# Small attention matmuls packed four at a time into PE tiles, in a linear-attention and MLP block

## The chip, the cores and the metric

One core of a Trainium2 chip. The metric is the device time of one execution in microseconds (us). Single executions are quoted as the median of a kernel's runs. "PE" is TensorE, "PEld" its weight loads, "DVE" VectorE, "ACT" ScalarE, "POOL" GpSimd, "SP" SyncE.

## The reference

The input is 2048 tokens of 640 features, bf16. After a layer norm, two branches are added to the input: a linear attention with 32 heads of 20 features, and a gated MLP with 1536 hidden features.

```python
q, k, v = split(xn @ wqkv)                       # 32 heads of 20
pq = einsum("bhsd,hdf->bhsf", q, w_phi); pk = same of k
phi_q = concat([softmax(pq), softmax(-pq)])      # 40 features a head
phi_k = concat([softmax(pk), softmax(-pk)])
kv  = einsum("bhsf,bhsd->bhfd", phi_k, v)        # the key-value sums, over all tokens
z   = einsum("bhsf->bhf", phi_k)
num = einsum("bhqf,bhfd->bhqd", phi_q, kv)       # the attention products
den = einsum("bhqf,bhf->bhq", phi_q, z)[..., None] + 1e-6
out = x + (num / den) @ wo + (silu(xn @ w1) * (xn @ w3)) @ w2
```

Two steps are awkward for matmuls of 128 x 128 tiles (the 128*128 of the page): both `kv` and `num` are 32 independent products of width 20, in two signs.

## The kernel before

A small scheduler, run while the program is built, records every instruction through one helper (hence one source line, L101, in all profile lines; L105 in the changed kernel) and fixes the order on each engine. MLP chunks (10 matmuls of 512 columns, 2.16 us of PE) fill PE wherever the attention has to wait.

The key-value sums take three heads as the stationary operand (63 columns, with a column of ones per head for `z`) in two column tiles of the array, 120 moving columns each. What is not on the diagonal of heads is thrown away later by a mask, after PE transposes have turned the result.

```python
def kv_sum(pairs, k):
    for n, p in enumerate(pairs):
        groups = [g for g in (2 * p, 2 * p + 1) if 3 * g < H]
        for t in range(T):                       # 16 token tiles of 128
            for g in groups:
                q, nh = g % 2, min(3, H - 3 * g)
                o = PS[64 * q:64 * q + 21 * nh, ...]       # column tile q
                mm(o, v2[:, t, 63 * g:63 * g + 21 * nh],
                   ekt[:, t, :, 60 * g:60 * g + 20 * nh], t == 0, t == T - 1, ...)
    ...                                          # copies to stg

def kv_store(chunks, k):
    ...
            tr(PSb[:, c:c + 128], stg[:, sg, 128 * fc:128 * fc + 128])   # PE transposes
    ...                                          # masked into KVc by DVE

def q_tok(t, k):                                 # attention products of one token tile
    for sg in range(2):
        for fc in range(DC):                     # 5 chunks of 128 features
            ...
                    mm(bank(k + 2 * sg + q, 22 * (hi - lo), ...),
                       EqT[b % 2][:, sg, fc, 128 * j:128 * j + 128],
                       KVc[:, sg, fc, ...], ...)           # full array, 154 or 88 columns
```

The softmax here doesn't subtract the row's maximum and nothing guards it: scores larger than these inputs give would overflow.

## Time and profile before

276.78 us median of 3 runs (276.57 to 276.87); the profiled execution spans 274.9 us.

First the head of the profile's page for the kernel before: busy time of PE and DVE, PE's busy tenths in 40 slices of the span, the instruction queue (packets, MB, share), and the head of the chain of waits.

```profile
span 274.9 us, 4782 instructions
PE 268.9 (98%) x1961; PEld 163.3 (59%) x1961; DVE 181.9 (66%) x318; ACT 108.1 (39%) x197; POOL 60.5 (22%) x93
PE   6999999999999999999999999999999999999996
q8 instruction: 15, 0.25, 0.4%
PE 81%; DMA 7%; DVE 5%; SPq 2%; ACT 2%; issue 1%; POOL 1%
```

PE is never out of work after the start, and in the order of time the chain is PE alone from 49.6 to 272.4 us. So a change is worth what it takes out of PE's time, or puts into it.

PE's timeline of the kernel before around the two steps: start us, length us, engine, line, operation, output<-inputs, shapes, count, and in brackets idle time before, if any.

```profile
85.60 4.96 PE L101 MATMUL PS<-ekt,v 128*63 128x120 bf16 x176
90.59 0.51 PE L101 MATMUL PS<-ident,stg 128*128 128x128 bf16 x6
90.94 2.32 PE L101 MATMUL PS<-xnT,w_s 128*128 128x512 bf16 x10
93.10 0.39 PE L101 MATMUL PS<-ident,stg 128*128 128x128 bf16 x4
93.32 8.80 PE L101 MATMUL PS<-xnT,w_s 128*128 128x512 bf16 x40
101.95 0.86 PE L101 MATMUL PS<-KVc,EqT 128*128 128x154 bf16 x12
102.65 2.32 PE L101 MATMUL PS<-xnT,Wqp 128*128 128x512 bf16 x10
```

Take starts, not lengths: matmuls overlap (at 512 columns each is 379 ns long and they start 216 ns apart), so what one group costs is the time to the next group's start. The key-value sums with their ten transposes cost 5.65 us: from 85.51, when the next ordinary matmul would have started, to 90.94, and 93.10 to 93.32. The attention products of one tile cost 102.65 - 101.95 = 0.70 us, 11.2 us for 16 tiles.

### The profile page before, as it was taken

What the parts mean: (1) busy time and instruction counts of PE and PEld (TensorE: products, weight loads), DVE (VectorE), ACT (ScalarE), POOL (GpSimd) and SP (SyncE); (2) the same over time, 40 slices, a digit from 0 to 9 for tenths busy, and PEclk for the clock granted to TensorE, in tenths of its full rate; (3) what the DMA queues carried; (4) which work ended last, traced back from release to release, by engine and by line L of the source; (5) the groups of instructions that cost most, each with busy time, mean ns of one, the idle gap of its engine ahead of it and who ended that gap; (6) DMA issues with size and microseconds to landing.
All of it is one profiled execution on the core that took longest, in us unless ns stands there. A gap on an engine that the chain in (4) does not pass through costs nothing.

```text
span 274.9 us, 4782 instructions
## 1 busy us (share of the span) xinstructions
PE 268.9 (98%) x1961; PEld 163.3 (59%) x1961; DVE 181.9 (66%) x318; ACT 108.1 (39%) x197; POOL 60.5 (22%) x93
## 2 busy tenths in 40 slices
PE   6999999999999999999999999999999999999996
PEld 2656666676447555555555455567446777777774
DVE  5459869999764698999899799978963121111112
ACT  2567987987821335445554544411320000000000
POOL 4404493999984100000000000000000000000000
DMA  7971899650000731111112111232300212121211
GB/s 202 296 223 37 176 244 295 115 145 0 0 0 2 222 117 24 25 24 26 24 31 43 24 25 26 49 46 52 93 5 0 89 56 82 61 84 61 81 42 48
DMA packets 40326, 21.96 MB, mean 80 GB/s; under 512 B 26736, under 2 KB 40304, under 8 KB 40304
## 3 DMA queue, kind: packets, MB, share of 16 engines
q1 hardware_dynamic: 40304, 21.66, 31.9%
q8 instruction: 15, 0.25, 0.4%
q14 instruction: 7, 0.06, 0.1%
HBM read 12.81 MB, written 2.62 MB: 56 GB/s over the span
## 4 chain that ended last, share of the span: by engine, by line
PE 81%; DMA 7%; DVE 5%; SPq 2%; ACT 2%; issue 1%; POOL 1%
PE PS L101 81%; DMA wqkT<-in_A_wqkv_dram 4%; DVE bst L101 3%; DMA x_tok<-in_A_x_dram 3%; SPq L113 2%; ACT x_tok L101 1%; DVE mv L101 1%; POOL rstd L101 1%; ACT ekt L101 0%; DVE Wkp L101 0%; DVE hT L101 0%; DVE t L101 0%; ACT v L101 0%; DVE xres L101 0%; DVE x_tok L101 0%
## 5 line engine op out<-in xcount | busy, mean ns | idle before, releaser
L101 PE MATMUL PS<-xnT,w_s 128*128 128x512 bf16 x480 | 107.2, 379 | 0.1
L101 PEld LDWEIGHTS PS<-xnT,w_s 128*128 128x128 bf16 x480 | 46.8, 98 | 55.1 <-ACT Wkp L101 0.3
L101 PE MATMUL PS<-w_s,hT 128*128 128x320 bf16 (+2 forms) x384 | 54.9, 299 | 0.0
L101 DVE TENSOR_TENSOR xres<-PS,xres 128x640 bf16<-128x640 f32 (+2 forms) x17 | 13.4, 786 | 54.0 <-PE PS L101 54.0
L101 ACT ACTIVATE th<-PS 128x512 f32<-128x512 f32 x48 | 28.7, 598 | 46.8 <-PE PS L101 46.8
L101 PEld LDWEIGHTS PS<-w_s,hT 128*128 128x128 bf16 x384 | 37.6, 98 | 14.6
L101 DVE SCALAR_TENSOR_TENSOR t<-th,PS 128x512 bf16<-128x512 f32 x48 | 32.7, 682 | 15.4 <-ACT th L101 15.4
L101 POOL TENSOR_TENSOR ekt<-ekt,rS 128x640 bf16<-128x640 bf16 x32 | 39.4, 1271 | 4.1 <-DVE rS L101 4.1
L101 DVE SCALAR_TENSOR_TENSOR hT<-t,PS 128x512 bf16<-128x512 bf16 x48 | 33.0, 687 | 1.7
L101 PE MATMUL PS<-wv,xnT 128*128 128x320 bf16 x160 | 24.7, 299 | 1.0 <-ACT xnT L101 1.0
L101 ACT ACTIVATE EqT<-PS 128x512 bf16<-128x512 f32 x40 | 21.7, 595 | 9.9 <-PE PS L101 9.9
L101 PE MATMUL PS<-wo_s,oT 128*128 128x320 bf16 (+2 forms) x160 | 24.5, 299 | 0.0
L101 DVE TENSOR_TENSOR prod<-PS,g_s 128x1280 bf16<-128x1280 f32 x16 | 23.9, 1491 | 0.5
L101 PE MATMUL PS<-Wkp,xnT 128*128 128x320 bf16 x160 | 23.9, 299 | 0.1
L101 PE MATMUL PS<-xnT,Wqp 128*128 128x512 bf16 x100 | 23.7, 379 | 0.0
L101 ACT ACTIVATE ekt<-PS 128x640 bf16<-128x640 f32 x32 | 20.8, 717 | 6.0 <-PE PS L101 6.0
L101 DVE TENSOR_REDUCE S<-ekt 128x64 f32<-128x1280 bf16 x16 | 23.0, 1441 | 0.0
L101 PEld LDWEIGHTS PS<-wv,xnT 128*128 128x128 bf16 x160 | 15.2, 98 | 7.5 <-ACT xnT L101 1.5
L101 PEld LDWEIGHTS PS<-Wkp,xnT 128*128 128x128 bf16 x160 | 15.4, 98 | 6.4 <-ACT ekt L101 0.3
L101 PEld LDWEIGHTS PS<-wo_s,oT 128*128 128x128 bf16 x160 | 15.6, 98 | 6.1
L101 DVE BATCH_NORM_STATS2 bst<-x_tok 128x6 f32<-128x320 bf16 x32 | 15.3, 478 | 5.8 <-DMA x_tok<-in_A_x_dram 5.2
L101 ACT ACTIVATE e_s<-PS 128x64 f32<-128x64 f32 x32 | 9.1, 283 | 22.0 <-PE PS L101 21.0
(53 smaller groups left out, 162.4 us busy)
## 6 DMA issues: line engine op xcount, KB each, us to landing
w_s<-in_B_w_dram SPq DMA_DIRECT2D x6, 640.0 KB, 6.7
xres<-in_A_x_dram SPq DMA_DIRECT2D x16, 160.0 KB, 2.4
out_dram<-xres SPq DMA_DIRECT2D x15, 160.0 KB, 1.8
x_tok<-in_A_x_dram SPq DMA_DIRECT2D x3, 640.0 KB, 6.2
w_s<-in_B_w_dram SPq DMA_DIRECT2D x1, 1920.0 KB, 8.0
wv<-in_A_wqkv_dram SPq DMA_DIRECT2D x2, 400.0 KB, 4.6
wo_s<-in_A_wo_dram SPq DMA_DIRECT2D x1, 800.0 KB, 4.7
x_tok<-in_A_x_dram SPq DMA_DIRECT2D x4, 160.0 KB, 2.9
```

Source lines behind the costliest of these rows:

```text
L101: o = _Op(eng, lambda: m(*args, **kw), r, w, cost)
L113: o = _Op(eng, lambda: m(out, in_), self.regions(in_), self.regions(out), nbytes, True)
```

## The change

The intent: give each 32-wide piece of work its own quarter of the array, so that four small matmuls run at once (as in the warm-up of the kernel before, where the four of a group start within 9 to 15 ns and each is 186 to 199 ns long in the profile) and nothing off the diagonal of heads is computed. The query features are permuted when the folded weight is written, so that 8 heads (160 features) lie as five blocks in each 32-row strip. The key-value sums of a head are one matmul of 21 x 40 in one of four 32-column tiles; one DVE 32 x 32 block transpose turns all of them and replaces the ten PE transposes. Small schedule edits go with it: the products of a token tile wait until the transposes of earlier tiles' results are at most two behind, and those transposes get priority.

```diff
+        if which:
+            evac(Wkp[...], bank2(k, 320))
+        else:
+            evac(Wqp[:, dc, :].rearrange("p (i b r j) -> p b r i j", b=2, r=2, j=32), ...)   # permuted
-    def kv_sum(pairs, k):
...
+    def kv_sum(k):
+        for n in range(8):
             for t in range(T):
+                for r in range(4):
+                    h = 8 * r + n
+                    o = PS[32 * r:32 * r + DH + 1, k * 512 + 40 * n:k * 512 + 40 * n + 40]
+                    mm(o.rearrange("p (s f) -> p s f", s=2), v2[:, t, 21 * h:21 * h + DH + 1],
+                       ekt[:, t, :, DH * h:DH * h + DH], t == 0, t == T - 1, ...)
...
+    def kv_store():
+        P.op("DVE", "transpose", [o], [i], (o, i), cost=0.5)
+        ...                                      # five masked products into KVc, for ten transposes and 15 products
     def q_tok(t, k):
         for sg in range(2):
-            for fc in range(DC):
-                ...
+            for i in range(DC):
+                for r in range(4):
+                    mm(bank(k + r, 22 * n, 176 * sg + 22 * h0),
+                       EqT[b % 2][32 * r:32 * r + 32, sg, i, 128 * j:128 * j + 128],
+                       KVc[32 * r:32 * r + 32, sg, i, 0:22 * n], ...)
```

The sums go from 176 matmuls to 512, the products from 12 a tile to 40. Each matmul is two PE instructions, a weight load and a matmul (1961 of each in the page before).

More of the change, by code (lines that the diff above doesn't have):

```diff
@@ L22, with heads_of_strip @@
 GRAN = 32
+def heads_of_strip(i):
+    return (32 * i) // DH, (32 * i + 31) // DH
 def heads_of_chunk(c):
@@ L288, in bass_parallel_sum__linear_kernel_hedgehog__glu_gated_swiglu__prompt_kernel @@
     den_s = new("den_s", [128, 2, H], f32)
-    g_s = new("g_s", [128, 2, 2, H], f32)
+    g_s = new("g_s", [128, 2, 4, 2, 8], f32)
     S64 = new("S64", [128, 3, 64], f32)
@@ L328, in bass_parallel_sum__linear_kernel_hedgehog__glu_gated_swiglu__prompt_kernel @@
     wqkT = new("wqkT", [128, 2 * DC, D], bf, RW)
-    KVc = new("KVc", [128, 2, DC, 9 * 22], bf, RW)
-    stg = new("stg", [128, 2, D], bf, RW + 3968)
-    prod = new("prod", [128, 2, 2, D], bf, RW + 3968)
+    KVc = new("KVc", [128, 2, DC, 3 * 22], bf, RW)
+    stg = new("stg", [128, 2, 160], bf, RW + 1344)
+    kvT = new("kvT", [128, 2, DC, 32], bf, RW + 1984)
+    SM = new("SM", [128, DC, 8], bf, RW + 2624)
+    prod = new("prod", [128, 2, 4, 2, 160], bf, RW + 3968)
     o_tok = new("o_tok", [128, 3, D], bf, RW + 9088)
@@ L434, in consts_late @@
         memset("POOL", eps[:, 0:1], 0.0)
-        for p in (20, 41, 62, 84, 105, 126):
-            select(eps[:, 0:1], -p, [[0, 1]], 1, ALU.not_equal, DEN_EPS / 2)
+        for r in range(4):
+            select(eps[:, 0:1], -32 * r - DH, [[0, 1]], 1, ALU.not_equal, DEN_EPS / 2)
         memset("POOL", v2[:].rearrange("p t (h c) -> p t h c", c=21)[:, :, :, DH], 1.0)
@@ L503, in fold_mm @@
                     first[q] = False
-        dst = (Wqp, Wkp)[which]
-        evac(dst[:, dc, :].rearrange("p (b c) -> p b c", c=320), bank2(k, 320))
+        if which:
+            evac(Wkp[:, dc, :].rearrange("p (b c) -> p b c", c=320), bank2(k, 320))
+        else:
+            evac(Wqp[:, dc, :].rearrange("p (i b r j) -> p b r i j", b=2, r=2, j=32),
+                 bank2(k, 320).rearrange("p b (r i j) -> p b r i j", r=2, j=32))
     def proj(t, w, k):
@@ L541, in k_norm @@
                ALU.mult)
-    def kv_sum(pairs, k):
-        for n, p in enumerate(pairs):
-            groups = [g for g in (2 * p, 2 * p + 1) if 3 * g < H]
+    def kv_sum(k):
+        for n in range(8):
             for t in range(T):
-                for g in groups:
-                    q, nh = g % 2, min(3, H - 3 * g)
-                    o = PS[64 * q:64 * q + 21 * nh, k * 512 + 120 * n:k * 512 + 120 * n + 40 * nh]
-                    first, last = n == 0 and t == 0, p == pairs[-1] and t == T - 1
-                    mm(o.rearrange("p (s f) -> p s f", s=2), v2[:, t, 63 * g:63 * g + 21 * nh],
-                       ekt[:, t, :, 60 * g:60 * g + 20 * nh], t == 0, t == T - 1, True,
-                       (0.09 if first or last else 0.0) + (0.0265 if len(groups) == 2 else 0.053))
-        full = [p for p in pairs if 6 * p + 6 <= H]
-        for q in range(2):
-            i = PS[64 * q:64 * q + 63, k * 512:k * 512 + 120 * len(full)]
-            o = stg[64 * q:64 * q + 63, :, 120 * full[0]:120 * full[0] + 120 * len(full)]
-            kv_copy(o.rearrange("p s (n q f) -> p n s q f", q=2, f=60)[:, :, :, q, :],
-                    i.rearrange("p (n s f) -> p n s f", s=2, f=60), eps[64 * q:64 * q + 63, 0:1])
-        if len(full) < len(pairs):
-            c = k * 512 + 120 * len(full)
-            kv_copy(stg[0:42, :, 600:640], PS[0:42, c:c + 80].rearrange("p (s f) -> p s f", s=2),
-                    eps[0:42, 0:1])
@@ new lines, in kv_sum @@
+                for r in range(4):
+                    h = 8 * r + n
+                    o = PS[32 * r:32 * r + DH + 1, k * 512 + 40 * n:k * 512 + 40 * n + 40]
+                    edge = r == 0 and (n == 0 and t == 0 or n == 7 and t == T - 1)
+                    mm(o.rearrange("p (s f) -> p s f", s=2), v2[:, t, 21 * h:21 * h + DH + 1],
+                       ekt[:, t, :, DH * h:DH * h + DH], t == 0, t == T - 1, True,
+                       (0.1 if edge else 0.0) + 0.0055)
+        kv_copy(stg[:].rearrange("p s (n f) -> p n s f", f=DH),
+                bank(k, 320).rearrange("p (n s f) -> p n s f", s=2, f=DH), eps[:, 0:1])
@@ L567, in kv_copy @@
     def kv_copy(o, i, e):
         n = free(o)
-        a = P.free["ACT"] + 0.17 + n / 1200
-        d = P.free["DVE"] + 0.14 + n / 960
-        if a <= d:
-            P.op("ACT", "activation", [o], [i, e], (o, i, ACT.Identity), dict(bias=e), cost=0.17 + n / 1200)
-        else:
-            P.op("DVE", "tensor_scalar", [o], [i, e], (), dict(out=o, in0=i, scalar1=e, scalar2=None,
-                 op0=ALU.add), cost=0.14 + n / 960)
-    def kv_store(chunks, k):
-        for n, fc in enumerate(chunks):
-            for sg in range(2):
-                c = k * 1024 + 256 * n + 128 * sg
-                tr(PSb[:, c:c + 128], stg[:, sg, 128 * fc:128 * fc + 128])
-        for n, fc in enumerate(chunks):
-            g0 = heads_of_chunk(fc)[0] // 3
-            ps = PSb[:, k * 1024 + 256 * n:k * 1024 + 256 * n + 256].rearrange("p (s c) -> p s c", s=2)
-            for g in range(g0, min(g0 + 3, 11)):
-                nh = min(3, H - 3 * g)
-                i = ps[:, :, 64 * (g % 2):64 * (g % 2) + 21 * nh].rearrange("p s (h c) -> p s h c", c=21)
-                o = KVc[:, :, fc, 66 * (g - g0):66 * (g - g0) + 22 * nh]
-                o = o.rearrange("p s (h c) -> p s h c", c=22)
-                m = GM[:, fc, 3 * g:3 * g + nh]
-                tt("DVE", o[:, :, :, 0:DH + 1], i,
-                   m.unsqueeze(1).unsqueeze(3).to_broadcast([128, 2, nh, DH + 1]), ALU.mult)
-            nh = min(9, H - 3 * g0)
-            o = KVc[:, :, fc, 0:22 * nh].rearrange("p s (h c) -> p s h c", c=22)[:, :, :, DH + 1]
-            copy("POOL", o, GM[:, fc, 3 * g0:3 * g0 + nh].unsqueeze(1).to_broadcast([128, 2, nh]))
@@ new lines, in kv_copy, with kv_masks @@
+        P.op("ACT", "activation", [o], [i, e], (o, i, ACT.Identity), dict(bias=e), cost=0.17 + n / 1200)
+    def kv_masks():
+        memset("POOL", SM[:], 1.0)
+        for r in range(4):
+            m = SM[32 * r:32 * r + 32, :, :]
+            select(m, 0, [[32, DC], [-DH, 8]], 1, ALU.is_ge, 0.0)
+            select(m, DH, [[-32, DC], [DH, 8]], -1, ALU.is_gt, 0.0)
+    def kv_store():
+        i, o = stg[:].rearrange("p s m -> p (s m)"), kvT[:].rearrange("p s i c -> p (s i c)")
+        P.op("DVE", "transpose", [o], [i], (o, i), cost=0.5)
+        for i in range(DC):
+            h0, h1 = heads_of_strip(i)
+            n = h1 - h0 + 1
+            o = KVc[:, :, i, 0:22 * n].rearrange("p s (h c) -> p s h c", c=22)
+            m = SM[:, i, h0:h1 + 1].unsqueeze(1)
+            tt("DVE", o[:, :, :, 0:DH + 1],
+               kvT[:, :, i, 0:DH + 1].unsqueeze(2).to_broadcast([128, 2, n, DH + 1]),
+               m.unsqueeze(3).to_broadcast([128, 2, n, DH + 1]), ALU.mult)
+            copy("POOL", o[:, :, :, DH + 1], m.to_broadcast([128, 2, n]))
@@ L610, in q_tok @@
         for sg in range(2):
-            first = [True, True]
-            for fc in range(DC):
-                h0, h1 = heads_of_chunk(fc)
-                g0 = h0 // 3 * 3
-                for q in range(2):
-                    lo, hi = max(h0, 16 * q), min(h1 + 1, 16 * q + 16)
-                    if lo < hi:
-                        mm(bank(k + 2 * sg + q, 22 * (hi - lo), 22 * (lo - 16 * q)),
-                           EqT[b % 2][:, sg, fc, 128 * j:128 * j + 128],
-                           KVc[:, sg, fc, 22 * (lo - g0):22 * (hi - g0)],
-                           first[q], fc == DC - 1 or (q == 0 and fc == 2), True)
-                        first[q] = False
-        ps = PS[:, k * 512:(k + 4) * 512].rearrange("p (n c) -> p n c", c=512)[:, :, 0:352]
-        ps = ps.rearrange("p n (h c) -> p n h c", c=22)
+            for i in range(DC):
+                h0, h1 = heads_of_strip(i)
+                n = h1 - h0 + 1
+                for r in range(4):
+                    edge = r == 0 and (sg == 0 and i == 0 or sg == 1 and i == DC - 1)
+                    mm(bank(k + r, 22 * n, 176 * sg + 22 * h0),
+                       EqT[b % 2][32 * r:32 * r + 32, sg, i, 128 * j:128 * j + 128],
+                       KVc[32 * r:32 * r + 32, sg, i, 0:22 * n],
+                       sg == 0 and i == 0, sg == 1 and i == DC - 1, True,
+                       (0.1 if edge else 0.0) + 0.0068)
+        ps = PS[:, k * 512:(k + 4) * 512].rearrange("p (r c) -> p r c", c=512)[:, :, 0:352]
+        ps = ps.rearrange("p r (h c) -> p r h c", c=22)
         e = e_s[:, t % 2, :, :]
         for sg in range(2):
-            act(e[:, sg:4 - sg:3 - 2 * sg, :].rearrange("p c (q h) -> p q h c", h=16),
-                ps[:, 2 * sg:2 * sg + 2, :, 20:22], ACT.Copy)
-        pr, den, g = pr_s[:, t % 2, :, :], den_s[:, t % 2, :], g_s[:, t % 2, :, :]
+            act(e[:, sg:4 - sg:3 - 2 * sg, :].rearrange("p c (r h) -> p r h c", h=8),
+                ps[:, :, 8 * sg:8 * sg + 8, 20:22], ACT.Copy)
+        pr, den, g = pr_s[:, t % 2, :, :], den_s[:, t % 2, :], g_s[:, t % 2, :, :, :]
         tt("DVE", pr, e[:, 0:2, :], e[:, 2:4, :], ALU.mult)
@@ L632, in q_tok @@
         P.op("DVE", "reciprocal", [den], [den], (den, den), cost=0.42)
-        tt("DVE", g, e[:, 2:4, :], den.unsqueeze(1).to_broadcast([128, 2, 32]), ALU.mult)
-        g = g.rearrange("p s (q h) -> p (s q) h", h=16)
-        p2 = prod[:, t % 2, :, :]
-        tt("DVE", p2.rearrange("p s (q h c) -> p (s q) h c", q=2, c=DH), ps[:, :, :, 0:DH],
+        tt("DVE", g.rearrange("p r s h -> p s r h"), e[:, 2:4, :].rearrange("p s (r h) -> p s r h", h=8),
+           den.rearrange("p (r h) -> p r h", h=8).unsqueeze(1).to_broadcast([128, 2, 4, 8]), ALU.mult)
+        g = g.rearrange("p r s h -> p r (s h)")
+        p2 = prod[:, t % 2, :, :, :]
+        tt("DVE", p2.rearrange("p r s (h c) -> p r (s h) c", c=DH), ps[:, :, :, 0:DH],
            g.unsqueeze(3).to_broadcast([128, 4, 16, DH]), ALU.mult)
-        tt("DVE", o_tok[:, t % 3, :], p2[:, 0, :], p2[:, 1, :], ALU.add, 2)
+        tt("DVE", o_tok[:, t % 3, :].rearrange("p (r c) -> p r c", r=4), p2[:, :, 0, :], p2[:, :, 1, :],
+           ALU.add, 2)
     nmlp = [0]
@@ L786, in attention @@
             yield None
-        yield lambda: memset("POOL", stg[:], 0.0)
-        yield lambda: kv_sum((0, 1, 2, 3), banks(1))
-        yield lambda: kv_sum((4, 5), banks(1))
-        yield lambda: kv_store((0, 1, 2), banks(1))
-        yield lambda: kv_store((3, 4), banks(1))
+        yield kv_masks
+        yield lambda: kv_sum(banks(1))
+        yield kv_store
         done["kv"] = 1
@@ L797, in attention @@
                 t = 4 * b + j
+                while done["o"] < t - 2:
+                    yield None
                 yield lambda t=t: q_tok(t, 0)
@@ L825, in bass_parallel_sum__linear_kernel_hedgehog__glu_gated_swiglu__prompt_kernel @@
     MLPS = 7
-    URGENT = {0: 4.0, 4: 4.0}
+    URGENT = {0: 4.0, 4: 4.0, 6: 4.0}
     streams = [norms(), transposes(), fold_k(), attention(), k_norms(), loads(), o_transposes(), mlps(), outs()]
```

## The prediction

> **What bounds it.** TensorE. The page gives PE 98% busy, the chain of waits gives it 81% of the span, and from 49.6 us to 272.4 us that chain is PE alone. There matmuls start at their streaming pitch, 216 ns for 512 columns. So only PE time taken out, or PE waits put in, count; DVE is busy 66%.
>
> **PE time concerned, before** (starts of matmuls in the timeline).
> - Key-value sums: 176 matmuls in two column tiles; a pair of 120 columns takes 53 ns. From when the previous 512-column matmul would have yielded (85.51) to the next one (90.94): 5.43 us, with six transposes in it. Four more transposes take 0.22 us. Sum 5.65 us.
> - Attention products: 12 matmuls per token tile, 101.95 to 102.65 us: 0.70 us, times 16 = 11.2 us.
>
> Together 16.9 us, 6% of the span.
>
> **After.** PE matmuls go from 1961 to 2735, but the small ones overlap four at a time. The kernel's own warm-up shows the rate: 32 matmuls of 66 columns in four 32-row tiles start within 240 ns, 29 ns per four[...]. The price is the change of tiling mode. [...]134 ns between the last two-tile and the first four-tile matmul of the warm-up, 93 ns above the pitch on entering the key-value sums, plus 25 ns at the first pair. I take 0.13 us per switch.
> - Attention products: 10 groups of four (44 or 66 columns), about 26 ns each (estimate), plus two switches: 0.52 us. Saved 0.18 us x 16 = 2.9 us.
> - Key-value sums: 128 groups of four 40-column matmuls at about 22 ns (estimate[...]), 2.8 us, plus two switches, 0.26. No PE transposes. They begin one MLP chunk (2.16 us) earlier, and need the POOL memset of v's ones column, which landed at 84.5; two selects fewer (0.33 us each) bring it to about 83.9, while PE arrives at about 83.4: a new wait of 0.4 us. Sum 3.5 us, saved 2.1 us.
>
> DVE's block transpose and POOL's masks are off the critical path. The order of instructions also shows 30 MLP chunks in one run before the first attention product, and output tiles, not MLP, between the later ones. Output tiles stay about five behind, so transposes should be hidden; I allow 0.2 us of new waits.
>
> **Sum:** 276.8 - 2.9 - 2.1 + 0.2 = about 271.8 us; I say 271.7 (-1.8%), 80% range 270.2 to 275.5. Faster by over 2%: 0.36; within 2%: 0.60; slower: 0.04.
>
> **What would show it.** Right: attention products 0.45 to 0.58 us a tile, gaps of 0.1 to 0.15 us beyond the pitch at either end; key-value sums about 2.8 us from first to last start; PE idle before them under 0.7 us; no other PE waits.
>
> **What would make it wrong.** (1) The sums are 1024 instructions in a row; the warm-up's burst was short enough to have been queued beforehand, so it proves no sustained rate. The trace shows PE's instructions arriving in 16 KB packets of about 1 us, one per some 256 instructions[...]. If fetch or decode cannot keep up, the sums take 5 to 12 us and the gain falls to 3 us or nothing. (2) Switches of 0.1 us or less: 271 or below. (3) All four banks are now needed at the first product; if DVE frees them late, PE waits once per tile in the output phase.

What the 26 and 22 ns for four matmuls were made of: by columns alone, the warm-up's 29 ns per four of 66 columns would be about 23 ns for the products (53 columns on average) and 17.6 ns for the sums (40 columns), estimates from that figure; the 3 and 4.4 ns above that were my allowance, which no trace showed. The 0.13 us per switch rests on the 134 ns of the warm-up. That the warm-up's burst could have been queued beforehand rests on its being over at 5.4 us, before the first packet on q8, PE's instruction queue, started (14.45 us).

## More of the kernel before

The granted clock is the share of full TensorE speed that the profile shows as allowed.

## The result, and the profile after

280.99 us median of 4 runs (280.10 to 282.09); the kernel before, with one more run on the same chip, 276.82 us (276.57 to 277.78). The ratio is 1.0144, 95% interval 1.0112 to 1.0176: 1.4% slower, where 1.8% faster was predicted. A ratio here is the mean time of one kernel's fast runs over that of the other's of the same rounds, so not quite the ratio of the medians quoted.

The same parts of the page for the changed kernel, with one row that the page before did not have: PEclk, the granted clock in tenths.

```profile
span 278.4 us, 6314 instructions
PE 263.4 (95%) x2711; PEld 155.8 (56%) x2735; DVE 179.4 (64%) x306; ACT 104.7 (38%) x196; POOL 60.9 (22%) x99
PE   6999999999994599999999999999999999999996
PEclk9999999999999599999999999999999999999999
q8 instruction: 21, 0.34, 0.5%
PE 88%; issue 4%; DMA 4%; SPq 2%; DVE 1%; ACT 1%
```

The loss is in one place, slices 13 and 14: PE is half idle, and in the second of them the clock is at half. All other slices of PE are as before. PE's timeline there:

```profile
83.51 1.30 PE L105 MATMUL PS<-ekt,v 128*21 128x40 bf16 x141
86.21 1.19 PE L105 MATMUL PS<-ekt,v 128*21 128x40 bf16 x128 [1.39 <-issue]
89.66 1.21 PE L105 MATMUL PS<-ekt,v 128*21 128x40 bf16 x128 [2.26 <-issue]
93.39 1.15 PE L105 MATMUL PS<-ekt,v 128*21 128x40 bf16 x115 [2.52 <-issue]
94.87 11.42 PE L105 MATMUL PS<-xnT,w_s 128*128 128x512 bf16 x48 [0.33 <-issue]
```

The 512 sums come in bursts of 141, 128, 128 and 115, with gaps (1.39, 2.26 and 2.52 us idle) that are released by "issue", that is by nothing the profile shows: no semaphore was waited for. 128 matmuls are 256 instructions. The page's instruction queue q8 moved 15 packets of 16 KB before and 21 after. With 3951 and about 5500 PE records that is one packet per 256 PE instructions, so q8 is PE's. The packets' start times, read from the trace, beside the bursts:

```
packet on q8 starts    83.83   87.34   90.83     (each lasts about 1.1 us)
burst resumes          86.21   89.66   93.39
```

Each burst resumes 2.3 to 2.6 us after a packet's start, and the next packet starts 1.1 to 1.2 us after that. A full turn takes 3.45 to 3.73 us for 256 instructions, while the array runs through them in about 1.1 us.

From 83.42, when the next ordinary matmul would have started, to 94.44, when the MLP resumes (its first record is missing), the sums took 11.0 us instead of 5.65: +5.4 us. The granted clock was 0.50 from 89.85 to 96.67 us; in the last 2.2 us of that the MLP's matmuls started 427 ns apart instead of 216, which lost another 1.1 us. The view of busy time by stretch shows clock and idle together (columns: stretch, its length, busy us and count of PE, PEld, DVE, ACT and POOL, granted clock, DMA share, GB/s):

```profile
87.40:89.66 2.26, 0.00 (x0) 0.00 (x0) 0.00 (x0) 0.00 (x0) 0.00 (x0) 1.00 0.00 0
89.66:90.87 1.21, 1.21 (x128) 1.10 (x128) 0.00 (x0) 0.00 (x0) 0.00 (x0) 0.58 0.06 14
90.87:93.39 2.52, 0.00 (x1) 0.00 (x0) 0.00 (x0) 0.00 (x0) 0.00 (x0) 0.50 0.00 0
94.50:96.50 2.00, 1.67 (x9) 0.70 (x6) 0.00 (x0) 0.53 (x1) 0.00 (x0) 0.50 0.36 47
```

In the second and third gap every engine is idle and no DMA runs but the instruction packet itself: nothing in the profile competes with it. (In the first, POOL still builds masks, 0.49 us.)

The attention products did what was predicted. One of the four tiles without a missing record:

```profile
236.84 0.46 PE L105 MATMUL PS<-KVc,EqT 32*128 32x44 bf16 x40
237.23 1.53 PE L105 MATMUL PS<-wo_s,oT 128*128 128x320 bf16 x10
```

237.23 - 236.84 = 0.39 us to the next group, plus 0.096 us on entry (the start of the first of them is that much later than the pitch of the matmul before it): 0.49 us a tile. Where 512-column matmuls follow it is 0.50. Against 0.70 that saves about 0.20 us, 3.1 us in 16 tiles. (After 12 of the tiles the record of the next 512-column matmul is missing from this trace, and the profile shows 0.16 us of idle that was not there; in a second trace of a kernel with the same products, e6_gap3 below, the records are complete and the exit takes 0.12 us everywhere.)

The balance: +5.4 + 1.1 - 3.1 = +3.4 us; the spans differ by 3.45. That holds for the two profiled executions, and the changed kernel's is the fastest of its four; the medians differ by 4.2. Its four runs rank as their mean granted clocks: 280.10 us at 0.988, 280.78 at 0.987, 281.20 at 0.981, 282.09 at 0.976. So in the others the clock was probably at half for longer (estimate: 0.976 of the 280.4 us span of the slowest is 13.5 us at 0.50, where the profiled run had 6.83) and cost more than 1.1 us; they have no trace here to show it.

### The profile page after: what moved, and what is told of

It is laid out like the page before. It is cut to its first block, busy times and chain, and to the rows that moved or that the text cites. A ratio compares the mean times of both kernels' runs of the same rounds, so it can differ in the third digit from the quotient of the medians.

```text
span 278.4 us, 6314 instructions
## 1 busy us (share of the span) xinstructions
PE 263.4 (95%) x2711; PEld 155.8 (56%) x2735; DVE 179.4 (64%) x306; ACT 104.7 (38%) x196; POOL 60.9 (22%) x99
## 4 chain that ended last, share of the span: by engine, by line
PE 88%; issue 4%; DMA 4%; SPq 2%; DVE 1%; ACT 1%
PE PS L105 88%; DMA wqkT<-in_A_wqkv_dram 4%; SPq L117 2%; DVE S L105 1%; ACT Wkp L105 0%; ACT ekt L105 0%; DVE t L105 0%; DVE rS L105 0%; DVE xres L105 0%; DVE hT L105 0%
## 5 line engine op out<-in xcount | busy, mean ns | idle before, releaser
L105 PE MATMUL PS<-xnT,w_s 128*128 128x512 bf16 x469 | 105.1, 381 | 1.0 <-issue 0.3
L105 PEld LDWEIGHTS PS<-w_s,hT 128*128 128x128 bf16 x384 | 37.6, 98 | 14.6
L105 ACT ACTIVATE e_s<-PS 128x64 f32<-128x64 f32 x32 | 6.4, 283 | 52.2 <-PE PS L105 52.2
L105 PE MATMUL PS<-xnT,Wqp 128*128 128x512 bf16 x87 | 20.9, 379 | 2.0 <-issue 1.9
```

Source lines behind the costliest of these rows:

```text
L105: o = _Op(eng, lambda: m(*args, **kw), r, w, cost)
```

## The experiments

Theory A: PE's instructions arrive a packet of 256 at a time, at most about one packet per 3.5 us; the sums' 1024 instructions in a row outrun it. Rival B: the gaps belong to the new matmuls themselves (column tiles, accumulation in PSUM, the data they wait for). Rival C: a packet boundary costs its time whatever runs meanwhile.

### e1_shift: move the packet boundaries, leave the sums alone

```diff
-        for n, cols, rep in ((2, 88, 10), (4, 66, 8)):
+        for n, cols, rep in ((2, 88, 10), (4, 66, 14)):     # 24 more warm-up matmuls, at 5 us
```

> The changed kernel with 24 more warm-up matmuls (48 instructions) at the very start, where PE idles anyway; nothing else moves. Theory A (PE's instructions arrive a 16 KB packet, 256 instructions, at a time, and the 1024-instruction run of key-value sums outruns the arrival): the gaps inside the sums, in the changed kernel after matmuls 141, 269 and 397 of 512, move by 24: none or a small one after 117, and gaps of 2 to 2.7 us after 245, 373 and 501; about the same total, 280 to 283 us. Rival B (the gaps belong to the data, to the accumulation in PSUM or to the column tiles): they stay after 141, 269 and 397.

280.82 us (one run). PE's timeline of e1_shift:

```profile
82.91 2.17 PE L105 MATMUL PS<-ekt,v 128*21 128x40 bf16 x245
87.62 1.25 PE L105 MATMUL PS<-ekt,v 128*21 128x40 bf16 x128 [2.54 <-issue]
91.08 1.25 PE L105 MATMUL PS<-ekt,v 128*21 128x40 bf16 x128 [2.20 <-issue]
94.53 0.28 PE L105 MATMUL PS<-ekt,v 128*21 128x40 bf16 x11 [2.21 <-issue]
```

The gaps stand after 245, 373 and 501, each exactly 24 matmuls earlier than a boundary of the changed kernel or its continuation (269, 397, 525). Matmuls added 78 us earlier moved them, so B falls. No gap stands after 117: the packet before had started long before, at 76.7, while long matmuls were still running.

### e2_half: half of the sums

```diff
-            for t in range(T):
+            for t in range(T // 2):        # wrong result on purpose
```

> The changed kernel with the key-value sums over 8 of the 16 token tiles (256 matmuls instead of 512; a wrong result on purpose). Theory A: only the gap after matmul 141 is left, about 1.6 us; the sums take 3.9 us instead of 11.0, the half-clock stretch goes, total 272 to 273.5 us. Rival B (a cost that goes with each matmul, 21.5 ns on average): the sums take 5.5 us, total 275 to 276 us.

273.68 us (one run), just above the range: only the gap after 141 is left.

```profile
83.59 1.31 PE L105 MATMUL PS<-ekt,v 128*21 128x40 bf16 x141 [0.30 <-POOL SM L105]
86.90 1.15 PE L105 MATMUL PS<-ekt,v 128*21 128x40 bf16 x115 [2.00 <-issue]
```

From start to start the gap is 2.2 us, more than expected, with PE late at the sums in this run (the profile puts 0.30 us of waiting down to POOL; the memset of v's ones column landed at 83.54), and the packet late too. The whole stage took 4.85 us, not 3.9. I had expected the half-clock stretch to go; it only shrank, to 3.4 us. So here it followed a single gap of 2.2 us.

### e4_rowburst: the kernel before, with a burst that has nothing to do with the sums

```diff
+    def row_burst():
+        for n in range(128):
+            for i in range(4):
+                mm(bank(i, 40), Wqp[32 * i:32 * i + 32, 0, 0:128], Wqp[32 * i:32 * i + 32, 1, 0:40], True, True)
...
         yield lambda: kv_store((3, 4), banks(1))
+        yield row_burst
```

> The kernel before, with 512 idle matmuls of 40 columns in four 32-row tiles put in one run after its key-value sums (each starts and stops by itself, nothing is accumulated, the result is not used and the output stays right). Theory A: they come in bursts of 128 with gaps of 2 to 2.7 us between them, take 8 to 11 us in all and add as much to the total, 285 to 288 us. Rival B (column tiles or accumulation make the gaps): 512 x 6 to 8 ns, 3 to 4 us with the switches, total 280 to 281 us.

292.82 us (one run), 15.7 more than the kernel before (277.14). Row tiles, no accumulation, other data: and again bursts of 128, with gaps of 5.3, 2.4 and 2.7 us from start to start, after 191, 319 and 447. The timeline up to 106 us, and two lines of the view by stretch (columns as above):

```profile
93.57 1.72 PE L101 MATMUL PS<-Wqp 32*128 32x40 bf16 x191
100.39 1.25 PE L101 MATMUL PS<-Wqp 32*128 32x40 bf16 x128 [5.09 <-issue]
103.84 1.25 PE L101 MATMUL PS<-Wqp 32*128 32x40 bf16 x128 [2.20 <-issue]
94.00:96.00 2.00, 1.29 (x156) 1.19 (x144) 1.57 (x5) 0.00 (x0) 0.53 (x2) 1.00 1.07 383
96.00:98.00 2.00, 0.00 (x0) 0.00 (x0) 1.57 (x5) 0.00 (x0) 0.26 (x1) 0.78 1.10 367
```

The burst took 14.5 us from first to last start, more than expected, and the clock was at half until 110.79, which slowed the MLP after it by about 1.3 us more (estimate: half of the 2.5 us from its first start, 108.25). It is the first gap that exceeds the expectation. It fell where the load of `w2` had all DMA engines busy (share 1.07 and 1.10 from 94 to 98 us), and the packet started only at 97.97, when that load was nearly over (its packets start at the full rate until 98.5). That the load held the packet up is argued from this, not tested.

### e5_wide: slow matmuls in the same burst

```diff
-                       ekt[:, t, :, DH * h:DH * h + DH], ...
+                       ekt[:, t, :, 160 * r:160 * r + 120], ...     # 240 columns for 40, wrong sums on purpose
...                                    # the output is widened to 240 columns too
```

> The changed kernel, its key-value sums still 512 matmuls in one run, but each with 240 moving columns instead of 40 (wrong sums on purpose), so that four take about 102 ns and 128 of them about 3.3 us, near the 3.45 to 3.7 us at which instruction packets came in the changed kernel. Theory A (execution hides the arrival, and the slower of the two sets the pace): gaps of 0.5 us or less, the sums take 13 to 14 us although they stream 9.9 us more than before, no half-clock stretch, total 281 to 284 us. Rival C (each packet boundary costs its 1.6 to 2.7 us whatever runs meanwhile): 19 to 20 us for the sums, total 288 us or more.

282.76 us (one run).

```profile
83.89 10.91 PE L105 MATMUL PS<-ekt,v 128*21 128x240 bf16 x397
95.07 3.15 PE L105 MATMUL PS<-ekt,v 128*21 128x240 bf16 x115 [0.27 <-issue]
```

Only the last gap is long enough to split the timeline. The three gaps shrank from 1.6, 2.5 and 2.7 us to 0.40, 0.26 and 0.53 (starts of matmuls, of which 0.09 is the usual pitch between groups of four); no half-clock stretch followed (the one that this trace has, 7.4 to 10.8 us, lies in the start phase, as in e6_gap3). From first to last start the sums took 14.1 us against 10.8, although every matmul streamed six times as many columns. C falls: here 128 matmuls took about 3.5 us (14.1 us by four), as long as a turn of the packets in the changed kernel (3.45 to 3.73 us), and execution hid the arrival; in the changed kernel 128 took about 1.1 us, and the arrival set the pace.

### e3_spread4: the same sums in four runs

```diff
-    def kv_sum(k):
-        for n in range(8):
+    def kv_sum(k, heads):
+        for n in heads:
...
-        yield lambda: kv_sum(banks(1))
+        held[0] = True                     # bank 7 is kept for the sums meanwhile
+        for n in range(0, 8, PER):         # PER = 2
+            m = nmlp[0] + GAP              # GAP = 2 MLP chunks between
+            while n and nmlp[0] < m:
+                yield None
+            yield lambda n=n: kv_sum(7, range(n, n + PER))
+        held[0] = False
```

> The changed kernel with the same 512 sums in four runs of 128 matmuls (256 instructions), two MLP chunks (4.3 us of PE) between the runs, in one PSUM bank kept for them. Theory A: no gap over 0.3 us within the sums and no half-clock stretch; each run takes about 1.1 us of PE with its two mode switches plus 0.2, all four 4.2 to 4.6 us instead of 11.0; total 272 to 274 us, 1 to 1.7% faster than the kernel before. Rival B: a gap of 1.5 to 2.5 us per 128 matmuls stays, total 280 us or more.

274.09 us median of 4, ratio to the kernel before 0.9891 (0.9870 to 0.9911): faster than both kernels. No half-clock stretch followed the sums. My "no gap over 0.3 us" was wrong, as its timeline shows:

```profile
83.06 1.20 PE L105 MATMUL PS<-ekt,v 128*21 128x40 bf16 x128
88.61 1.14 PE L105 MATMUL PS<-ekt,v 128*21 128x40 bf16 x121
90.54 0.22 PE L105 MATMUL PS<-ekt,v 128*21 128x40 bf16 x7 [0.80 <-issue]
95.12 1.20 PE L105 MATMUL PS<-ekt,v 128*21 128x40 bf16 x128
100.67 1.20 PE L105 MATMUL PS<-ekt,v 128*21 128x40 bf16 x128
```

The packet that ended this gap started at 88.24, just before the second run began: PE had only just passed the boundary before, and resumed 2.30 us after the packet's start. The sums cost 5.9 us of PE time in all.

### e6_gap3 and e7_spread8: the spacing

```diff
-    PER, GAP = 2, 2
+    PER, GAP = 2, 3        # e6_gap3
+    PER, GAP = 1, 1        # e7_spread8
```

> As e3_spread4, with three MLP chunks (6.5 us) between the runs instead of two. In e3_spread4 one gap of 0.99 us was left, where the second run met a packet boundary 2.4 us after the previous one had been passed. Theory A: no gap over 0.3 us, the sums with their switches take 4.8 to 5.1 us of PE time instead of 5.9, total 272.8 to 273.6 us, 1.2 to 1.6% faster than the kernel before. If it is no faster than e3_spread4, the remaining gap was not what I take it for.

> As e3_spread4, with eight runs of 64 matmuls and one MLP chunk between. Theory A: no gap, since a packet now lasts over 4 us, but four more visits to the column-tiled mode at about 0.22 us each: sums with switches 5.8 to 6.2 us, total 273.6 to 274.6 us, between e6_gap3 and the kernel before.

e6_gap3: 272.99 us median of 4, ratio 0.9841 (0.9782 to 0.9900; the interval is wide because one run of the kernel before took 280.26 us, one reason why e10_gap3_again repeats it below). PE's timeline has no idle time left around the sums, which cost 4.95 us with their eight switches:

```profile
83.92 1.19 PE L105 MATMUL PS<-ekt,v 128*21 128x40 bf16 x128
85.04 6.65 PE L105 MATMUL PS<-xnT,w_s 128*128 128x512 bf16 x30
91.62 1.20 PE L105 MATMUL PS<-ekt,v 128*21 128x40 bf16 x128
92.75 6.65 PE L105 MATMUL PS<-xnT,w_s 128*128 128x512 bf16 x30
99.32 1.20 PE L105 MATMUL PS<-ekt,v 128*21 128x40 bf16 x128
```

e7_spread8: 274.38 us median of 4 (273.65 to 275.64), ratio 0.9890 (0.9812 to 0.9969), no gap either, but four more visits to the tiled mode. By its trace the sums cost 5.6 us, under the 5.8 to 6.2 expected and 0.6 more than in e6_gap3; the medians differ by 1.4. The other 0.8 us is not explained, and its runs spread by 2.0 us.

### e8_body2 and e9_switch2: what the attention products consist of

```diff
-        for sg in range(2):
+        for sg in (0, 1, 0, 1):                          # e8_body2
...
+            if sg == 0:                                  # e9_switch2: a full-array matmul in the middle
+                mm(bank(k, 40, 400), EqT[b % 2][:, 0, 0, 128 * j:128 * j + 128], KVc[:, 0, 0, 0:40], False, False, True)
```

> e6_gap3 with the 40 attention matmuls of every token tile issued twice in the same visit to the row-tiled mode (the second pass starts the sums afresh, the result stays right). By the trace of the changed kernel the body takes 0.28 us a tile and the two switches 0.22: if so, 16 x 0.28 = 4.5 us more than e6_gap3, 277 to 278 us. If the body were a larger part of the 0.50 us, or packets ran late here too, 279 us or more.

> e6_gap3 with one idle full-array matmul of 40 columns in the middle of each tile's attention products, so that the array leaves the row-tiled mode and comes back once more per tile (the result stays right). If two switches cost 0.22 us and the matmul 0.02 to 0.03 us: 16 x 0.25 = 4 us more than e6_gap3, 276.5 to 277.5 us. If the mode costs nothing and the 0.22 us is the ordinary start and end of any group of small matmuls: 273.5 us or less.

> e6_gap3 again, to pair with the two runs of this call and because a run of the kernel before was odd (280.3 us) in the earlier call: 272.8 to 273.6 us, 1.2 to 1.6% faster than the kernel before.

e10_gap3_again: 272.68 us median of 4, ratio 0.9853 (0.9825 to 0.9881): 1.5% faster than the kernel before.

e9_switch2: 276.79 us (2 runs, 276.02 and 277.56), 4.1 us more than e10_gap3_again. In its trace the stretch from first to last product of a tile grew from 0.281 to 0.506 us: leaving the mode and coming back, with the small matmul, costs 0.225 us, or 3.6 us in 16 tiles; two runs do not resolve the other 0.5. The rival of the expectation (the mode costs nothing, 273.5 us or less) falls: one interruption costs about what entry and exit together do. What the full-array weight load takes of it was not separated from the change of mode.

e8_body2: 278.53 us (2 runs), 5.9 us more, not 4.5, and above the 277 to 278 expected. The second pass of 40 matmuls took 0.334 us where the first took 0.281, and no packet gap stands in it: in a longer stretch the matmuls start every 8.3 ns. The sums of the changed kernel show the same pace inside a burst: the first eight groups of four start about 25 ns apart (2 to 6 ns between the four), and from then on matmuls start singly, every 8 to 9 ns, 33 ns per four. It is the same for 40 columns in column tiles as for 44 and 66 in row tiles, so it goes with the number of matmuls, or of their instructions; what sets it is left open.

## Why the prediction was wrong, point by point

- **PE bounds the kernel, DVE and POOL do not matter: right.** Every microsecond gained or lost was PE time.
- **Attention products 0.52 us a tile, 2.9 us saved: right.** 0.49 to 0.50 us, 3.1 us saved. Of the two parts, the body took 0.28 us for 0.26 and the switches 0.21 to 0.22 for 0.26, so two small errors nearly cancel.
- **0.13 us per mode switch: a little high.** 0.096 on entry, 0.12 on exit; e9_switch2 gives 0.225 for a pair with a small matmul in it.
- **Key-value sums "at about 22 ns (estimate), 2.8 us", sum 3.5 us, saved 2.1 us: wrong, and this is the step that failed.** They took 11.0 us. Of the 7.5 us that were missed, 6.7 are three gaps for instruction packets (e1, e2, e4, e5); the pace of 33 ns per four instead of 22 adds 1.3, and the wait for POOL that did not come takes off 0.4. Even with no gap at all the sums would have gained about 1.3 us, not 2.1; e6_gap3, with three more visits to the tiled mode, gains 0.7.
- **"If fetch or decode cannot keep up, the sums take 5 to 12 us and the gain falls to 3 us or nothing": the mechanism was named, but given too little weight.** The evidence before was enough to do better. The trace before showed 16 KB packets of 0.93 to 1.26 us, one per 256 PE instructions. The sums need four. One after another, four take about 4 us (estimate from those times), so 2.8 us could hold only if some lay ready beforehand or came side by side; the estimate assumed that without saying so. What the trace before could not show was the time from a packet's start until PE resumes, 2.3 to 2.6 us in the trace after, where a turn took 3.45 to 3.73 us although the packet itself took 1.1. The sums of the kernel before are 352 instructions in 4.96 us, 14 ns each; the supply in the changed kernel was 3.45 to 3.73 us for 256, 13.5 to 14.6 ns each. In the kernel before only two packets started near that stretch (82.87 and 89.57 us), so nothing showed.
- **The half clock: not foreseen.** It cost 1.1 us in the profiled run, after the gaps rather than in them. Stretches at 0.50 that came with gaps lasted 6.83 us in the changed kernel, 3.4 us in e2_half (one gap of 2.2 us) and 13.65 us in e4_rowburst (gaps of 5.3, 2.4 and 2.7 us); e3_spread4, with a gap of 1.0 us, had none (granted clock 1.000). How much idle time it takes was not measured.
- **A new wait of 0.4 us for POOL: not there in this trace, but by chance.** The memset landed at 82.80, before PE arrived at 83.42; its chain on POOL had also started about 1 us earlier. In e2_half the same memset landed at 83.54 and the sums started 0.37 us late: the wait was foreseen rightly as possible, and comes and goes between executions (the two kernels are the same up to there).
- **0.2 us of waits in the output phase: none seen.** The 12 idle times of 0.16 us there are missing records.

So the change holds one good idea and one that is spoilt by its own instruction count. With the sums spread, both together give 272.7 us; 3.8 of the 4.0 us gained over the kernel before are accounted for by the products (3.1) and the sums (0.7).

## What to carry to other kernels

Splitting matmuls into more, smaller ones turns array time into instructions (here 176 matmuls into 512, 352 instructions into 1024): before packing, divide the instructions of the densest stretch by its time and compare with what packets of instructions have been seen to deliver. Where a burst is too dense, mix it with long matmuls instead of running it alone; the gaps came from the density of the instructions and not from their total number, which is about the same in e6_gap3. The number has its own price: each small matmul in a long run took 8.3 ns here, whatever its width of 40 to 66 columns. And a short burst that ran fast says little about a long one: the warm-up that gave the rate had 32 matmuls and was over (5.4 us) before the first packet on q8 started (14.45 us in the trace before), and in the sums the first 32 took about 25 ns per four, the rest 33.
